# Order of the first layers and early casts in a retention and leaky-ReLU kernel

## The chip, the cores and the metric

The kernel runs on one core of a Trainium2 chip. Times are device microseconds of one execution; lower is better. Thirteen runs of the kernel before are shown, and one further look in detail, a profile of one of them. The engines are named as in the profile: PE multiplies matrices, DVE and POOL work elementwise, ACT does activations and copies, SP issues most of the transfers.

## What is computed

Two stages, one after the other. The first is a retention layer (attention without softmax): for each of 8 batches and 8 heads, with 576 positions and 64 channels,

```python
scores = scale * np.matmul(q, k.transpose(0, 1, 3, 2))
gamma = 1.0 - 2.0 ** (-5.0 - np.arange(H, dtype=np.float32))
Dmat = np.where(rel >= 0, gamma[:, None, None] ** rel[None, :, :], 0.0)
ret = scores * Dmat[None, :, :, :]
return np.matmul(ret, v)
```

Its output, seen as 4608 tokens of 512 channels, goes through two layers:

```python
h = x @ w_in                    # 512 -> 2048
g = np.maximum(0.01 * h, h)
return g @ w_out                # 2048 -> 512
```

Inputs and output are float32; the kernel multiplies in float16 and accumulates in float32.

## The kernel before

**Units and groups.** The 4608 tokens are 36 units of 128 tokens (two chunks of 64), and 9 groups of 512 tokens, four units each. A unit is what the retention stage works on; a group is what the two layers work on. Units 0 to 3 make group 0, units 4 to 7 group 1, and so on.

**A unit's life.** `load` (L119) fetches k, q and v, each 256 KB, into `t32` tiles, of which there are six for each of the three. `cast_k` (L170) rounds k to float16 on ACT; `cast_q` and `cast_v` (L174, L177) do so on DVE or POOL and multiply by the decay. q and k are then transposed, into `qkT`: either on PE with a copy out (`turn`, L624: `transpose_pe` and `transposed`), or by a DMA that SP issues (`transpose_dma`, L181). `scores` (L209) issues 64 small matmuls into one PSUM tile, `sc`: the scores and, beside them, each chunk's contribution to the running state. DVE masks the scores (`masks`) and adds the state to what is carried from chunk to chunk (`state`); `state_cast` rounds it, on DVE, ACT or POOL as the caller says.

**Two forms of a unit's output.** `outputs` (L283) puts the part inside a chunk and the part from the state into two halves of an `ot` tile; `own` (L353) copies the first half on ACT, and `add` (L359) adds the second to it on DVE, into the unit's 128 columns of `xT`, the input of the first layer. `outputs_acc` (L309) lets PE accumulate both parts in one half of the tile, with a drain of PE between its two rounds, and `x_copy` (L340) brings it to `xT` by one copy on ACT. There is one `ot` tile and one `sc` tile.

**The first layer** makes 16 blocks of 128 hidden channels for each group, through one of four `acc` accumulators, and ACT applies the leaky ReLU from there into `gt`. The blocks come in three shapes: `h_block` (L389), 512 tokens at a time; `h_half(g, a, fb)` (L394), two blocks for the half `a` of the tokens, and `halves` calls it for a list of (a, fb); `h_unit(u, fb)` (L401), four blocks for one unit alone. They let the first layer of groups 0 and 1 begin before all four units are there.

**The second layer.** Group 0 uses `wide` (L419), four PE calls of 16 matmuls for each 128 tokens. Groups 1 to 8 use `seven` (L469): a product by halves with seven multiplications instead of eight, as in Strassen's and Winograd's scheme. It needs differences of the weights (`mix_weights`, L440, once for all groups) and sums of the activations (`mix`, L455, parts 0 to 3 for each group), all on DVE. In `seven` p1 is a sum of two products in one accumulator; between the two, ACT copies p1 out (`keep`, L492, into `k1`), and p6 plus k1 gives u2, from which the rest follows. `give` (L499) writes an output half, and its store follows.

**Order.** Nothing is reordered: each engine runs its instructions in the order in which the source issues them. That order is written out by hand:

- the opening (L558 to L613): transfers are issued by SP and POOL; then units 0 to 3, each with `scores`, state, masks, the transposes of the next unit, and for units 0 to 2 the output. `keep_warm` (L546) issues matmuls on zeros, whose result nobody reads.
- groups 0 and 1 of the first layer (L639 to L693), with units 4 to 7 between their blocks.
- group 0 of the second layer (L751 to L754), during which the retention of units 8 and 9 runs: `burst` (L700) issues the scores of a unit and the outputs of the unit before it, `ahead` (L715) the casts and the DMA transpose of a later unit, and `early` (L734) a burst, an `ahead` three units on and a `load` five units on. The dictionary `at` says after which of the 16 `wide` calls each comes.
- `early(10)`, the last sums of group 1, and `seven(1, ...)` with `early(11)` after its first product and `early(12)` after its fifth.
- groups 2 to 8 (L761 to L776), with a `step` (burst, load, `ahead`) at four fixed places of each.

SP issues its transfers in the order of the source as well: the transpose of unit u stands between loads of later units. `load(8)` waits for the third of four transfers of `w_out`.

Of the kernel before, what the change touches and what calls it, by code (L numbers as in the profile page):

```python
# [18 lines left out]
def kernel(  # L19
# [125 lines left out]
    def load_w_in(f, after=None):  # L145
        fs = slice(f * FQ, (f + 1) * FQ)
        rows = moe_w_in.rearrange("(o c k) f -> o k c f", o=2, k=CH)
        ds = []
        for o in range(2):
            ds.append(nc.gpsimd.dma_start(out=w_in16[half(o), :, fs], in_=rows[o][:, :, fs]))  # L150
            if after is not None and not o:
                behind(ds[0], *after)
        return ds
# [16 lines left out]
    def cast_k(u):  # L170
        qk16[u] = a_pool.tile([P, 2, H, D], F16, name="qk16")
        nc.scalar.copy(out=qk16[u][:, 1], in_=t32[u, 1])  # L172
# [167 lines left out]
    def x_copy(u):  # L340
        nc.scalar.copy(  # L341
            out=x_of(u), in_=ot_tiles[u][:, 0].rearrange("q (c j) t -> q c (j t)", j=2)
        )
# [125 lines left out]
    def seven(g, hooks, last=False):  # L469

        r = {}
        s = sums[g]

        def product(name, lhs, rhs, fresh):
            if fresh:
                r[name] = acc_pool.tile([P, 2, HN], FP, name="acc")
            order = (
                [(f, tb) for tb in range(2) for f in range(HF)]
                if last
                else [(f, tb) for f in range(HF) for tb in range(2)]  # L480
            )
            for n, (f, tb) in enumerate(order):
                nc.tensor.matmul(  # L483
                    out=r[name][:, tb, :],
                    lhsT=lhs[:, f, tb * P : (tb + 1) * P],
                    rhs=rhs[:, f, :],
                    start=fresh and n == 0,
                    stop=f == HF - 1,
                    skip_group_check=True,
                )  # L490

        def keep(name, of, plus=None):  # L492
            r[name] = m_pool.tile([P, 2, HN], FP, name=name)
            if plus is None:
                nc.scalar.copy(out=r[name], in_=r[of])  # L495
            else:
                nc.vector.tensor_tensor(out=r[name], in0=r[of], in1=r[plus], op=ADD)

        def give(a, b, of, plus=None, parts=1):  # L499
            if ("o", a) not in r:  # L500
                r["o", a] = o_pool.tile([P, 2, DM], FP, name="osb")
            for n in range(parts):
                ts = slice(n * 2 // parts, (n + 1) * 2 // parts)
                to = r["o", a][:, ts, b * HN : (b + 1) * HN]
                if plus is None:
                    nc.scalar.copy(out=to, in_=r[of][:, ts])
                else:
# [12 lines left out]
            if r["n", a] == 2 and not (last and a == 1):  # L520
                store(g, a, r["o", a])

        plan = (
            ("p1", g_part(g, 0, 0), w_part(0, 0), True, lambda: keep("k1", "p1")),
            ("p1", g_part(g, 0, 1), w_part(1, 0), False, lambda: give(0, 0, "p1")),
            ("p6", s[:, 1], w_mix[:, 1], True, lambda: keep("u2", "p6", "k1")),
            ("p5", s[:, 0], w_mix[:, 0], True, lambda: keep("v", "p5", "u2")),
            ("p7", g_part(g, 1, 0), w_mix[:, 2], True, lambda: give(1, 1, "p7", "v")),
            ("p5", g_part(g, 0, 0), w_part(1, 1), False, lambda: give(0, 1, "p5", "u2")),
            (  # L530
                "p7", g_part(g, 1, 1), w_mix[:, 3], False,
                lambda: give(1, 0, "p7", "u2", 2 if last else 1),
            ),
        )
        for n, (name, lhs, rhs, fresh, then) in enumerate(plan):
            product(name, lhs, rhs, fresh)
            then()
            if n == 0:
                mix(g, 3, 0)
                mix(g, 3, 1)  # L540
            for f in hooks.get(n, ()):
                f()
# [17 lines left out]
    load(1, {1: nc.sync, 0: nc.gpsimd, 2: nc.gpsimd})  # L560
    load(2, nc.gpsimd)
    load(3, {1: nc.sync, 0: nc.gpsimd, 2: nc.gpsimd}, {1: (last_load[1, 1],)})
    for f in range(3):
        load_w_in(f)
    load(4, nc.gpsimd)
    load_w_in(3)
    for u in range(5, 8):
# [14 lines left out]
    for u in range(4):  # L582
        n = u + 1
        scores(u)
        if not u:
            keep_warm(3)
        state(u, 0)
        state_cast(u, dve_copy, (0,))
        masks(u)
        if not u:  # L590
            cast_q(1, nc.vector)
            cast_v(1, nc.vector)
        state(u, 1)
        if n < 4:
            transpose_pe(n, 1)
            transposed(n, 1, act_copy)
            if not u:
                keep_warm(3)
                outputs_acc(0)
                x_copy(0)  # L600
                keep_warm(1)
            transpose_pe(n, 0)
            transposed(n, 0, act_copy)
            keep_warm(2 if not u else 3)
        if n < 3:
            cast_k(n + 1)
            cast_q(n + 1, nc.vector)
            cast_v(n + 1, nc.vector)
        state_cast(u, act_copy, (1,))
        if 0 < u < 3:  # L610
            outputs_acc(u)
            x_copy(u)
            keep_warm(2)  # L613


    def halves(g, *items):
        for a, fb in items:
            h_half(g, a, fb)

    def cast_qv(u):  # L620
        cast_q(u, nc.vector)
        cast_v(u, nc.vector)

    def turn(u, x):  # L624
        transpose_pe(u, x)
        transposed(u, x, dve_copy)

    def settle(u):
        state(u, 0)
        state_cast(u, dve_copy, (0,))  # L630
        masks(u)
        state(u, 1)

    def finish(u):
        outputs_acc(u)
        x_copy(u)
        state_cast(u, act_copy, (1,))

    halves(0, (0, 0), (0, 1))  # L639
    outputs_acc(3)  # L640
    x_copy(3)
    halves(0, (0, 2), (0, 3), (1, 0))
    cast_k(4)
    cast_qv(4)
    halves(0, (1, 1), (1, 2), (1, 3))
    turn(4, 1)
    halves(0, (0, 4), (0, 5))
    turn(4, 0)
    halves(0, (1, 4), (1, 5))
    cast_k(5)  # L650
    scores(4)
    settle(4)
    cast_qv(5)
    halves(0, (0, 6), (0, 7))
    finish(4)
    turn(5, 1)
    cast_k(6)
    halves(0, (1, 6))
    turn(5, 0)
    halves(0, (1, 7))  # L660
    scores(5)
    settle(5)
    cast_qv(6)
    h_unit(4, 0)
    turn(6, 1)
    cast_k(7)
    h_unit(4, 1)
    finish(5)
    turn(6, 0)
    h_unit(5, 0)  # L670
    scores(6)
    settle(6)
    cast_qv(7)
    h_unit(5, 1)
    turn(7, 1)
    halves(1, (0, 4))
    finish(6)
    turn(7, 0)
    halves(1, (0, 5))
    scores(7)  # L680
    settle(7)
    halves(1, (0, 6), (0, 7))
    finish(7)
    load(8, after=(w_out_loads[2],))
    load(9)
    h_unit(6, 0)
    mix_weights(0, 0)
    mix_weights(0, 1)
    h_unit(7, 0)
    for n in range(1, 4):  # L690
        mix_weights(n, 0)
        mix_weights(n, 1)
        halves(1, (1, 2 * n), (1, 2 * n + 1))  # L693

    def mixes(g, *ns):
        for n in ns:
# [34 lines left out]
        ahead(u + 2)  # L731


    def early(u, out=True):  # L734
        burst(u, out)
        if 8 < u < 12:
            ahead(u + 3)
            load(u + 5)

    ahead(8)  # L740
    load(10)
    ahead(9)
    load(11)
    at = {
        2: lambda: (ahead(10), load(12)),
        4: lambda: (burst(8, False), ahead(11), load(13)),
        9: lambda: early(9),
        11: lambda: mixes(1, 0),
        13: lambda: mixes(1, 1),
    }  # L750
    for n in range(16):  # L751
        wide(n // 4, n % 4)
        if n in at:
            at[n]()  # L754
    early(10)
    mixes(1, 2)
    seven(1, {0: [lambda: early(11)], 4: [lambda: early(12)]})

    first = [f for i in range(4) for f in (i, i + HF)]
# [47 lines left out]
```

## Time and profile before

| | us |
|---|---|
| median of 13 runs | 301.19 |
| lowest and highest run | 296.9, 302.9 |
| the profiled execution | 302.66 |
| its span, first to last instruction | 300.9 |

All 13 runs, sorted: 296.9, 297.45, 298.21, 298.23, 299.72, 299.99, 301.19, 301.35, 301.48, 302.36, 302.64, 302.66, 302.9.

The page of the profiled execution opens with the busy time of each engine:

```profile
PE 285.3 (95%) x4096; PEld 193.7 (64%) x4096; DVE 169.6 (56%) x291; ACT 144.0 (48%) x254; POOL 103.8 (34%) x124
```

PEld is the load of weights, which overlaps PE's matmuls. Where the time of PE goes, by stretches of the span:

| stretch, us | what runs on PE | PE busy, us | mean clock | DMA share |
|---|---|---|---|---|
| 0 to 20 | opening: units 0 to 3, fillers | 15.99 | 1.00 | 1.02 |
| 20 to 50 | first layer of group 0, units 4 to 7, part of group 1 | 28.17 | 1.00 | 1.05 |
| 50 to 60 | first layer of group 1 | 9.91 | 1.00 | 0.34 |
| 60 to 70 | second layer of group 0, units 8 and 9 | 9.86 | 1.00 | 0.95 |
| 70 to 80 | the same, unit 10, first product of group 1 | 6.46 | 0.97 | 1.16 |
| 80 to 90 | unit 11, second layer of group 1 | 8.87 | 0.69 | 1.08 |
| 90 to 100 | the same, unit 12 | 10.00 | 1.00 | 1.14 |
| 100 to 284 | groups 2 to 8 | full | 1.00 | 0.10 to 1.09 |
| 284 to 301 | last second layer | 12.26 | 1.00 | 0.17 |

The clock is the share of full speed that was granted to PE; the DMA share is the mean busy share of the core's 16 DMA engines.

What one operation takes, from the groups of instructions: a first-layer matmul of 512 columns 0.216 us one after the other (64 in 13.81 us), of 256 columns 0.109, of 128 columns 0.056; an activation, a copy or a cast of 128 x 512 on ACT 0.58 to 0.62; an elementwise product of that size on DVE 0.68, on POOL 1.04; one load of 256 KB lands 3.8 to 5.1 us after its issue, one DMA transpose 3.2.

The chain of work that ended last, by engine:

```profile
PE 86%; DMA 5%; POOL 2%; SPq 2%; issue 2%; ACT 1%; DVE 1%; DVEq 0%; ACTq 0%; POOLq 0%
```

"SPq" is SP's queue of transfers; "issue" is time in which an engine waited for nothing that the profile shows.

### The profile page before, as it was taken

How to read it: one execution, taken by the hardware profiler on the slowest of the kernel's cores; microseconds unless marked ns; L12 is line 12 of the kernel's file. 1: busy time of each engine (PE TensorE's matmuls, PEld its weight loads, DVE VectorE, ACT ScalarE, POOL GpSimd, SP SyncE). 2: the span in 40 equal slices, each digit the busy share in tenths (PEclk: the TensorE clock that was granted, in tenths of full speed). 3: DMA queues.
4: the chain of work that ended last, by engine and by line, in shares of the span. 5: the costliest groups of instructions: out<-in, count | busy, mean ns of one | idle time of the engine just before them, and what ended most of it. 6: DMA issues, size and time to landing. Idle time of an engine off the chain costs nothing.

```text
span 300.9 us, 9407 instructions
## 1 busy us (share of the span) xinstructions
PE 285.3 (95%) x4096; PEld 193.7 (64%) x4096; DVE 169.6 (56%) x291; ACT 144.0 (48%) x254; POOL 103.8 (34%) x124
## 2 busy tenths in 40 slices
PE   7799989999499999999999999999999999999994
PEld 2468878745387458646864686478547844884583
DVE  2862469717925358555746664577358636740342
ACT  4547756712412762376147624761575166306510
POOL 8859503324442333333334333333334514000000
PEclk9999999999779999999999999999999999999999
DMA  8999999199999975996698767967896361012003
GB/s 222 272 240 240 239 198 200 26 190 202 165 297 228 285 154 133 219 237 136 132 246 196 181 143 219 178 156 171 220 215 139 69 176 37 4 45 97 0 2 139
DMA packets 132219, 50.01 MB, mean 166 GB/s; under 512 B 121777, under 2 KB 126513, under 8 KB 132177
## 3 DMA queue, kind: packets, MB, share of 16 engines
q1 hardware_dynamic: 125904, 39.73, 58.4%
q0 software_dynamic: 5984, 9.57, 14.4%
q8 instruction: 32, 0.52, 0.7%
q10 hardware_dynamic: 288, 0.11, 0.1%
q14 instruction: 11, 0.08, 0.1%
HBM read 36.81 MB, written 9.44 MB: 154 GB/s over the span
## 4 chain that ended last, share of the span: by engine, by line
PE 86%; DMA 5%; POOL 2%; SPq 2%; issue 2%; ACT 1%; DVE 1%; DVEq 0%; ACTq 0%; POOLq 0%
PE acc L373 42%; PE acc L483 33%; DMA t<-in_v_dram 4%; PE sc L215 3%; POOL t L132 2%; DMA t<-in_k_dram 1%; PE acc L423 1%; PE ot L321 1%; PE sc L224 1%; SPq L183 1%; PE ot L291 1%; PE ot L302 1%; PE acc L200 1%; SPq L132 1%; PE ot L333 1%
## 5 line engine op out<-in xcount | busy, mean ns | idle before, releaser
L373 PE MATMUL acc<-xT,w_in 128*128 128x512 f16 (+2 forms) x752 | 130.7, 329 | 0.6 <-ACT xT L341 0.3
L387 ACT ACTIVATE gt<-acc 128x512 f16<-128x512 f32 x144 | 85.9, 597 | 57.5 <-PE acc L373 56.0
L373 PEld LDWEIGHTS <-w_in 128*128 128x128 f16 x752 | 68.0, 98 | 52.4 <-issue 0.9
L483 PEld LDWEIGHTS <-gt 128*128 128x128 f16 x640 | 62.6, 99 | 11.7 <-issue 1.8
L233 DVE TENSOR_TENSOR s<-sc,cs 128x512 f16<-128x512 f32 x36 | 24.7, 685 | 43.9 <-PE sc L224 43.9
L483 PE MATMUL acc<-w_out,gt 128*128 128x256 f16 x384 | 47.6, 279 | 1.8 <-ACT k L495 1.6
L273 POOL CAST st<-s 128x512 f16<-128x512 f32 x21 | 13.7, 653 | 83.3 <-DVE s L257 53.7
L175 POOL TENSOR_TENSOR qk<-t,cs 128x512 f16<-128x512 f32 x28 | 29.3, 1047 | 33.3 <-DMA t<-in_q_dram 31.9
L355 ACT COPY own<-ot 128x512 f32<-128x512 f32 x28 | 16.4, 586 | 38.5 <-PE ot L302 31.2
L179 POOL TENSOR_TENSOR v<-t,cs 128x512 f16<-128x512 f32 x28 | 31.8, 1134 | 4.9 <-DMA t<-in_v_dram 4.4
L172 ACT CAST qk<-t 128x512 f16<-128x512 f32 x36 | 22.2, 620 | 21.6 <-DMA t<-in_k_dram 17.0
L483 PE MATMUL acc<-w_mix,gt 128*128 128x256 f16 x256 | 30.6, 273 | 0.0
L467 DVE TENSOR_TENSOR mix<-gt 128x1024 f16<-128x1024 f16 x16 | 14.0, 878 | 28.8 <-ACT gt L387 28.8
L483 PE MATMUL acc<-w_mix,mix 128*128 128x256 f16 x256 | 29.5, 274 | 0.0
L483 PEld LDWEIGHTS <-mix 128*128 128x128 f16 x256 | 25.2, 99 | 3.1
L360 DVE TENSOR_TENSOR xT<-ot,own 128x512 f16<-128x512 f32 x28 | 19.1, 682 | 1.6 <-ACT own L355 1.6
L257 DVE TENSOR_TENSOR s<-sc,s 128x256 f32<-128x256 f32 x40 | 16.7, 418 | 3.7 <-PE sc L224 2.6
L215 PEld LDWEIGHTS <-qkT 64*64 64x64 f16 x576 | 7.8, 108 | 15.1 <-issue 9.1
L508 DVE TENSOR_TENSOR osb<-acc,u 128x512 f32<-128x512 f32 (+1 forms) x17 | 11.1, 655 | 8.0 <-PE acc L483 8.0
L215 PE MATMUL sc<-qkT 64*64 64x64 f16 x576 | 11.6, 199 | 3.5 <-DMA qkT<-qk 3.1
L467 DVE TENSOR_TENSOR mix<-mix,gt 128x1024 f16<-128x1024 f16 x16 | 14.4, 905 | 0.5
L423 PE MATMUL acc<-w_out,gt 128*128 128x512 f16 x64 | 14.3, 379 | 0.0
(52 smaller groups left out, 234.4 us busy)
## 6 DMA issues: line engine op xcount, KB each, us to landing
out_dram<-osb SPq DMA_DIRECT2D x17, 512.0 KB, 3.7
t<-in_k_dram SPq DMA_DIRECT2D x28, 256.0 KB, 3.8
t<-in_q_dram SPq DMA_DIRECT2D x25, 256.0 KB, 4.1
t<-in_v_dram SPq DMA_DIRECT2D x25, 256.0 KB, 5.1
w_in<-in_moe_w_in_dram POOLq DMA_DIRECT2D x8, 256.0 KB, 7.2
w_out<-in_moe_w_out_dram POOLq DMA_DIRECT2D x4, 512.0 KB, 11.2
t<-in_v_dram POOLq DMA_DIRECT2D x7, 256.0 KB, 5.4
t<-in_q_dram POOLq DMA_DIRECT2D x6, 256.0 KB, 5.3
```

Source lines behind the costliest of these rows:

```text
L172: nc.scalar.copy(out=qk16[u][:, 1], in_=t32[u, 1])
L175: eng.tensor_tensor(out=qk16[u][:, 0], in0=t32[u, 0], in1=decay(u, 0), op=MUL)
L179: eng.tensor_tensor(out=v16[u], in0=t32[u, 2], in1=decay(u, 1), op=MUL)
L215: nc.tensor.matmul(out=a[half(j), g, 0, p, :], lhsT=qkT[u][half(g), 1, p, half(j)], rhs=qkT[u][half(g), 0, p, half(j)], start=True, stop=T ...
L233: nc.vector.tensor_tensor(out=s16s[u], in0=sc_tiles[u][:, :, 0], in1=mask_sb.unsqueeze(1).unsqueeze(1).to_broadcast([P, 2, NP, CH]), op=MUL,)
L257: nc.vector.tensor_tensor(out=to, in0=st, in1=carry[0], op=ADD)
L360: nc.vector.tensor_tensor(out=x_of(u).rearrange("q (c g) t -> q c g t", g=2), in0=ot_tiles[u][:, :, NP : 2 * NP].rearrange("q g (c j) t -> ...
L373: nc.tensor.matmul(out=hps[:, n, :], lhsT=w_in16[:, c, f * P : (f + 1) * P], rhs=xT[g][:, c, ts], start=(c == 0), stop=(c == NP - 1),)
L387: nc.scalar.activation(out=out, in_=in_, func=mybir.ActivationFunctionType.Lrelu)
L423: nc.tensor.matmul(out=ys[tb], lhsT=g_t[0][:, f, tb * P : (tb + 1) * P], rhs=w_out16[:, f, :], start=(f == 0), stop=(f == NF - 1),)
L467: nc.vector.tensor_tensor(out=z[:, fs], in0=a[:, fs], in1=b[:, fs], op=op)
L483: nc.tensor.matmul(out=r[name][:, tb, :], lhsT=lhs[:, f, tb * P : (tb + 1) * P], rhs=rhs[:, f, :], start=fresh and n == 0, stop=f == HF - ...
```

## The change

Five things are changed.

1. In the last group's `seven`, p6 is computed second, between the two products of p1.
2. In the opening, the two `keep_warm` matmuls after the outputs of unit 2 are left out. The loop is written with other conditions, and the order of what remains is the same.
3. Units 3 and 4 use `outputs`, `own` and `add` (a new function `finish2`) in place of `outputs_acc` and `x_copy`. Units 5 to 7 keep `finish`.
4. In the first layers of groups 0 and 1 the steps of units 4 to 7 stand at other places: `scores(4)` after `halves` (0, 4) instead of after (1, 5), the outputs of unit 4 three half blocks earlier, `cast_k(6)` after `settle(5)`, `finish(7)` after `h_unit(6, 0)`. Two half blocks of group 1, (1, 2) and (1, 3), become `h_unit(6, 1)` and `h_unit(7, 1)`.
5. `ahead(8)`, `load(10)`, `ahead(9)` and `load(11)` move from after the first layer of group 1 to between its last blocks, and `ahead(10)` with `load(12)` one `wide` call up. The sums 0, 1 and 2 of group 1 move from after the `wide` calls 11, 13 and the burst of unit 10 to after the calls 0, 3 and 7.

```diff
+        if last:
+            plan = (plan[0], plan[2], plan[1]) + plan[3:]
         for n, (name, lhs, rhs, fresh, then) in enumerate(plan):
...
-        if 0 < u < 3:
-            outputs_acc(u)
-            x_copy(u)
+        if u == 1:
+            outputs_acc(1)
+            x_copy(1)
             keep_warm(2)
+        elif u == 2:
+            outputs_acc(2)
+            x_copy(2)
...
+    def finish2(u):
+        outputs(u)
+        own(u)
+        add(u)
...
     halves(0, (0, 0), (0, 1))
-    outputs_acc(3)
-    x_copy(3)
+    finish2(3)
     halves(0, (0, 2), (0, 3), (1, 0))
     cast_k(4)
     cast_qv(4)
-    halves(0, (1, 1), (1, 2), (1, 3))
+    halves(0, (1, 1), (1, 2))
     turn(4, 1)
-    halves(0, (0, 4), (0, 5))
+    halves(0, (1, 3))
     turn(4, 0)
-    halves(0, (1, 4), (1, 5))
-    cast_k(5)
+    halves(0, (0, 4))
     scores(4)
     settle(4)
+    halves(0, (0, 5), (1, 4))
+    finish2(4)
+    state_cast(4, act_copy, (1,))
+    halves(0, (1, 5))
+    cast_k(5)
     cast_qv(5)
     halves(0, (0, 6), (0, 7))
-    finish(4)
     turn(5, 1)
-    cast_k(6)
     halves(0, (1, 6))
     turn(5, 0)
     halves(0, (1, 7))
     scores(5)
     settle(5)
+    cast_k(6)
     cast_qv(6)
...
     halves(1, (0, 6), (0, 7))
-    finish(7)
     load(8, after=(w_out_loads[2],))
     load(9)
     h_unit(6, 0)
+    finish(7)
+    h_unit(6, 1)
     mix_weights(0, 0)
     mix_weights(0, 1)
     h_unit(7, 0)
-    for n in range(1, 4):
-        mix_weights(n, 0)
-        mix_weights(n, 1)
-        halves(1, (1, 2 * n), (1, 2 * n + 1))
...
+    h_unit(7, 1)
+    mix_weights(1, 0)
+    mix_weights(1, 1)
+    halves(1, (1, 4))
+    ahead(8)
+    load(10)
+    mix_weights(2, 0)
+    mix_weights(2, 1)
+    halves(1, (1, 5), (1, 6))
+    ahead(9)
+    load(11)
+    mix_weights(3, 0)
+    mix_weights(3, 1)
+    halves(1, (1, 7))
...
-    ahead(8)
-    load(10)
-    ahead(9)
-    load(11)
     at = {
-        2: lambda: (ahead(10), load(12)),
+        0: lambda: mixes(1, 0),
+        1: lambda: (ahead(10), load(12)),
+        3: lambda: mixes(1, 1),
         4: lambda: (burst(8, False), ahead(11), load(13)),
+        7: lambda: mixes(1, 2),
         9: lambda: early(9),
-        11: lambda: mixes(1, 0),
-        13: lambda: mixes(1, 1),
     }
...
     early(10)
-    mixes(1, 2)
     seven(1, {0: [lambda: early(11)], 4: [lambda: early(12)]})
```

The functions `mixes`, `burst`, `ahead`, `fetch` and `step` are moved up in the file, unchanged.

More of the change, by code (lines that the diff above doesn't have):

```diff
@@ L562 @@
     load(3, {1: nc.sync, 0: nc.gpsimd, 2: nc.gpsimd}, {1: (last_load[1, 1],)})
-    for f in range(3):
-        load_w_in(f)
+    load_w_in(0)
+    load_w_in(1)
+    load_w_in(2)
     load(4, nc.gpsimd)
@@ L603 @@
             transposed(n, 0, act_copy)
-            keep_warm(2 if not u else 3)
+            keep_warm(3 if u else 2)
         if n < 3:
@@ L637, in finish @@
         state_cast(u, act_copy, (1,))
-    halves(0, (0, 0), (0, 1))
-    outputs_acc(3)
-    x_copy(3)
-    halves(0, (0, 2), (0, 3), (1, 0))
-    cast_k(4)
-    cast_qv(4)
-    halves(0, (1, 1), (1, 2), (1, 3))
-    turn(4, 1)
-    halves(0, (0, 4), (0, 5))
-    turn(4, 0)
-    halves(0, (1, 4), (1, 5))
-    cast_k(5)
[L651 to L654, printed above, removed]
-    finish(4)
-    turn(5, 1)
-    cast_k(6)
[L658 to L682, printed above, removed]
-    finish(7)
[L684 to L689, printed above, removed]
-    for n in range(1, 4):
-        mix_weights(n, 0)
-        mix_weights(n, 1)
-        halves(1, (1, 2 * n), (1, 2 * n + 1))
+    def finish2(u):
+        outputs(u)
+        own(u)
+        add(u)
     def mixes(g, *ns):
@@ L731, in step @@
         ahead(u + 2)
+    halves(0, (0, 0), (0, 1))
+    finish2(3)
+    halves(0, (0, 2), (0, 3), (1, 0))
+    cast_k(4)
+    cast_qv(4)
+    halves(0, (1, 1), (1, 2))
+    turn(4, 1)
+    halves(0, (1, 3))
+    turn(4, 0)
+    halves(0, (0, 4))
+    scores(4)
+    settle(4)
+    halves(0, (0, 5), (1, 4))
[3 more added lines that the diff above has]
+    cast_k(5)
+    cast_qv(5)
+    halves(0, (0, 6), (0, 7))
+    turn(5, 1)
+    halves(0, (1, 6))
+    turn(5, 0)
+    halves(0, (1, 7))
+    scores(5)
+    settle(5)
+    cast_k(6)
+    cast_qv(6)
+    h_unit(4, 0)
+    turn(6, 1)
+    cast_k(7)
+    h_unit(4, 1)
+    finish(5)
+    turn(6, 0)
+    h_unit(5, 0)
+    scores(6)
+    settle(6)
+    cast_qv(7)
+    h_unit(5, 1)
+    turn(7, 1)
+    halves(1, (0, 4))
+    finish(6)
+    turn(7, 0)
+    halves(1, (0, 5))
+    scores(7)
+    settle(7)
+    halves(1, (0, 6), (0, 7))
+    load(8, after=(w_out_loads[2],))
+    load(9)
+    h_unit(6, 0)
+    finish(7)
+    h_unit(6, 1)
+    mix_weights(0, 0)
+    mix_weights(0, 1)
+    h_unit(7, 0)
+    h_unit(7, 1)
[12 more added lines that the diff above has]
+    halves(1, (1, 7))
     def early(u, out=True):
```

## The prediction

> **What bounds the kernel now.** The page's first part comes first: PE is busy 285.3 us of a 300.9 us span (95%), so time is won where PE idles or is slowed, or where it does work the result doesn't need. The slices (7.5 us each, part 2) show where:
>
> ```profile
> PE   7799989999499999999999999999999999999994
> ...
> PEclk9999999999779999999999999999999999999999
> DMA  8999999199999975996698767967896361012003
> ```
>
> There are three low places: slices 0 to 5 (the opening), slice 10 with a low clock in slices 10 and 11 (75 to 90 us), and the last. DMA falls to 1 in slice 7 (52.7 to 60.2 us) and is full from slice 8: a hole just ahead of a shortage. Next the waits of PE after 60 us:
>
> ```profile
> PE sc L215 <- DMA qkT<-qk: 3.1, 1, 3.1
> PE acc L483 <- ACT k L495: 1.6, 2, 0.9
> PE ot L302 <- POOL st L273: 0.6, 2, 0.4
> ```
>
> That is nearly all PE waits for until the end; from 100 us on each group takes 29.1 us without a gap. PE's timeline places the 3.1:
>
> ```profile
> 79.96 0.43 PE L215 MATMUL sc<-qkT 64*64 64x64 f16 x16 [3.11 <-DMA qkT<-qk]
> ...
> 82.37 3.57 PE L483 MATMUL acc<-w_out,gt 128*128 128x256 f16 x16 [0.92 <-ACT k L495]
> ```
>
> The first is scores(11), waiting for unit 11's transpose. The second is p1's second product, which can't accumulate before ACT has copied p1 (`keep k1`). It took 3.57 us where sixteen of that shape take 1.92 elsewhere: clock 0.50 from 80 to 86 us by the two-microsecond windows. The chain of waits says why both are late:
>
> ```profile
> 66.83 5.49 DMA t<-in_v_dram
> ...
> 73.62 1.08 POOL st L273
> ...
> 76.69 4.43 DMA t<-in_k_dram
> ...
> 81.22 0.63 ACT qk L172
> ```
>
> SP, ACT and DMA carry it: k of unit 13 lands at 81.1, cast_k(13) stands on ACT ahead of k1's copy. SP's timeline has where this string of transposes (T) and loads (L) begins:
>
> ```profile
> 59.60 1.33 SPq L183 DMA_TRANSPOSE qkT<-qk  x1
> 61.03 0.53 SPq L132 DMA_DIRECT2D t<-in_k_dram  x1
> ```
>
> T8 59.6, L10 61.0, T9 63.2, L11 65.6, T10 68.3, L12 71.3, T11 74.1, L13 75.9: SP hardly rests in between, since each transfer takes 0.5 to 2.9 us to issue and DMA is full. T8 started only when ACT had cast k(8), and ACT shows that cast after the last activation:
>
> ```profile
> 58.42 0.60 ACT L387 ACTIVATE gt<-acc 128x512 f16<-128x512 f32 x1 [0.28 <-PE acc L373]
> 58.92 1.13 ACT L172 CAST qk<-t 128x512 f16<-128x512 f32 x2
> ```
>
> Unit 8's q had landed at 49.7 (POOL casts it there). So the whole string is about six microseconds later than its data allowed, because of its place in ACT's and SP's order.
>
> **What the Trainium skill says.** "TensorE: Matmul & The Clock Gate", section "What's actually happening": PE's clock is halved after an idle window of about 3.4 us and restored after as long a busy one. The trace agrees in kind, and 3.11 us of waiting were enough here: clock 0.50 from 80 to 86, back at 1.00 from 88. "DMA: Bandwidth & Descriptors", section "Issuing engines are not separate DMA queues": all queues share 16 DMA engines. The trace agrees in that share is about 1.0 from 64 us on; so the string can be started earlier, hardly run faster. "GPSIMD Engine Reference", section "1. Specifications": its SBUF interface is shared with VectorE. The trace agrees: the pair of w_mix subtractions under POOL's casts took 2.98 us, the last pair alone 1.28.
>
> **The change part by part.** The sum is made on the profiled execution: 302.66 us, span 300.9 and 1.76 around it.
>
> *(a) Fillers after outputs 2.* Two keep_warm matmuls go, 18.66 to 19.20: 0.53 us of PE. scores(3) starts at about 18.6; its inputs are ready (qkT copies end at 17.7, the sc bank is read out at 18.0). The first chunk of w_in had landed by 17 (POOL's waits on it), so first blocks start at 19.0, not 19.5.
>
> *(b) Plain outputs for 3 and 4.* outputs_acc(4) holds PE 34.26 to 35.03, 0.77 us with its drain; `outputs` takes 0.26 (a burst's 64 matmuls 0.64, less 0.38 for scores). Saved 0.5 each. But xT is then made by own on ACT (0.59) and add on DVE (0.69) in place of one 0.59 copy. For unit 4 many blocks cover that: 0.5 stays. For unit 3 it does not. ACT's queue (state cast, two activations, copy) hangs on scores(3): before, x_copy ended at 23.68; now own ends at about 23.15, add at 23.9. PE reaches block (1,0), the first that reads unit 3, at 19.0 + 1.85 + 0.26 + 1.75 = 22.85 and waits 1.1 us. It started (1,0) at 24.07 before, 23.95 now: of 1.0 us saved by (a) and unit 3, 0.1 is left.
>
> *(c) Order of units 4 to 7.* scores(4) and outputs(4) move up by three half blocks; cast_k(4) ends at 26.0 and q(4) at 25.6, ahead of their turns at 26.6 and 27.7. cast_k(6) now follows the last activation of group 0, and turn(6,1) may wait up to 0.15 us: I take 0.1. h_unit(6,1) and (7,1) replace two halves: 16 x 0.056 against 8 x 0.109, equal. finish(7) is one unit later, with the same 0.9 us block over its copy. In all (a) to (c): 0.1 + 0.5 - 0.1 = **0.5 us**. The 0.87 and 0.26 us gaps without a releaser in this stretch I leave as they are.
>
> *(d) Casts of 8 and 9 between blocks.* `ahead(8)` now comes after the fifth of eight blocks, three of 0.875 us earlier: T8 at 57.0 in PE's old time instead of 59.6, 2.6 us. ahead(9) comes one block before the end, done by 58.7, before T9's turn (60.6). Loads 8 and 9 don't change place; SP has issued them by 51.1, and load 8's wait for the third w_out transfer stays. ACT holds the sixth activation 0.3 us longer; four accumulators cover it. T8 also waits for POOL's cast_q(8), done at 50.8. In the string every L and T after that moves with T8: T11 lands at 77.3 (79.9), k(13) at 78.5 (81.1).
>
> *(e) mix 0 to 2 of group 1 earlier.* Six DVE instructions leave 71.5 to 79.1 for 59 to 66, where DVE had 3 us of work in 10 and POOL little: PE time 0. masks(8) at 63.1 come after the 2.6 us of the first four; if contention stretches these as it did w_mix they end near 63, still in time.
>
> Then PE: st(9) on POOL stood behind v(11) and held PE 0.43; moved by 2.6 this goes, and PE asks for scores(11) at 76.4. It waits until 77.3 (0.85), for st(10) until 78.4 (0.6), for k1, which stays behind cast_k(13), until 79.7 (1.1). p1's second product starts at 79.72 instead of 82.37: **2.65 us**. What is late next is still k(13). As no gap nears a window, I take the clock to stay up: before, that product lost 1.65 and p6 0.25, so **1.9 us**. If it still halves, 0; if stalls were short already, less.
>
> *(f) Last group, p6 second.* p1's second product waited 0.72 for k1. p6 needs the second sum, ready at 285.95 on DVE; PE starts at 286.05 instead of 286.34: **0.3 us**.
>
> Sum: 0.5 + 2.65 + 1.9 + 0.3 = 5.35; 302.66 - 5.35 = 297.3. The runs shown go from 296.9 to 302.9, median 301.19, 1.5 below the profiled one. No trace shows what varies; I suppose half is this stall, and take 0.8 off: **296.5 us**.
>
> **The rivals.**
> *Fully hidden.* If the string gets through faster (it has an idle DMA in front of it), the remaining 2.5 us of waits go as well: 297.3 - 2.5 = 294.8. For it: T took 1.3 us to issue when DMA was calm, 2.9 when full. Against: its data are the same.
> *No gain at the stall.* The string is limited by completions, not by its start, or the clock halves all the same: (d) pays 0 to 1, the rest 0.8: 301.19 - 0.8 - 0.5 = 299.9, within 1%. Against: DMA moved nothing from 54 to 60.
> *Slower, in the opening.* With fillers gone and 1.1 us of idleness ahead of (1,0), the clock halves at 23: 3.4 to 7 us at half speed cost 1.7 to 3.5, the wait 1.1, and if (d) pays nothing then 301.2 + 3 = 304. It decides once the gaps between 18.6 and 24 fill most of a window. Against: before, at 12 to 14, PE had 1.14 us of work in 2 and kept its clock.
> *Not what it says:* the built order shows ahead(8) between activations and SP's order unchanged, so I give this nothing.
>
> **How the numbers follow.** Likeliest 0.52 (296.5, from 295 to 298.2), fully hidden 0.22, no gain 0.18, slower 0.08. About 1% is what a measurement of this kernel tells from no change: 298.2 and 304.2. Faster by over 1%: 0.52 x 0.95 + 0.22 + 0.02 for part of the third, about 0.73; within: 0.21; slower 0.06. The range leaves out the slow case and the ends of the others: 293.9 to 299.6.
>
> **What would show it.** T8 should start about 3 us before the block that ends the first layer does, scores(11) wait under 1 us, PE's clock stay at 9 in all slices, k1's wait be the last left near 79. Block (1,0) should show about 1 us of waiting on DVE's add. In the last group the wait for k1 should be gone. I am wrong if T11 lands as late after T8 as PE arrives, or if a new low clock shows near 23 us.

## The result, and the profile after

| | us |
|---|---|
| changed kernel, median of 11 runs | 294.56 |
| its lowest and highest run | 293.08, 296.91 |
| the kernel before, median of 48 runs | 300.63 |
| ratio, 95% interval | 0.9845 (0.9812 to 0.9879) |
| the profiled execution of the changed kernel | 292.49 (span 290.7) |

The median is 6.1 us lower, which is a ratio of 0.980. The ratio in the table comes out nearer to 1, since it leaves out slow runs, those more than 1.5% above the fastest of their kernel: 15 of the 48 of before and one of the changed kernel. The two profiled executions lie 10.2 us apart, since that of before was one of its longer ones and that of the changed kernel is shorter than all 11 runs. So the two traces together overstate the change, and the sum below is checked against several traces of each kind.

The slices of the changed kernel, tenths of each 7.3 us:

```profile
PE   8898999999999999999999999999999999999994
...
PEclk9999999999999999999999999999999999999999
DMA  7999998699999998966697669889986151012003
```

The low place of PE in slice 10 is gone, and so is the low clock. DMA's hole is a 6 where it was a 1. What PE still waits for after 17 us, in this execution:

```profile
PE acc L373 <- DVE xT L360: 0.8, 1, 0.8
PE acc L373 <- ACT xT L341: 0.3, 1, 0.3
PE ot L321 <- ACT qkT L207: 0.3, 1, 0.3
PE acc L200 <- issue: 0.2, 1, 0.2
```

Neither scores(11), which waited 3.11 us before, nor k1 is in the list; the first line is block (1, 0), which waits for unit 3's add. SP's timeline has the string of transposes and loads (T8 is the transpose of unit 8, and so on):

```profile
54.62 1.32 SPq L183 DMA_TRANSPOSE qkT<-qk  x1
56.05 0.53 SPq L132 DMA_DIRECT2D t<-in_k_dram  x1
...
68.06 1.75 SPq L183 DMA_TRANSPOSE qkT<-qk  x1
```

T8, the first of these lines, is issued at 54.6, and T11, the last, at 68.1. PE begins group 0's second layer at 55.9, so T8 stands 1.24 us ahead of that, where it stood 1.38 behind: 2.62 us earlier. Here are ACT and PE at the place where p1's second product was slow before:

```profile
73.65 0.62 ACT L172 CAST qk<-t 128x512 f16<-128x512 f32 x1 [1.07 <-DMA t<-in_k_dram]
74.17 0.58 ACT L495 COPY k<-acc 128x512 f32<-128x512 f32 x1
```

```profile
74.81 1.91 PE L483 MATMUL acc<-w_out,gt 128*128 128x256 f16 x16
```

cast_k(13) still waits for its load and k1's copy still stands behind it, but both are over when PE gets there. In other executions of the same kernel they are not, as will be seen.

### The profile page after: what moved, and what is told of

Same layout as the page of the kernel before. It is cut to its first block, busy times and chain, and to the rows that moved or that the text cites. A ratio compares the mean times of both kernels' runs of the same rounds, so it can differ in the third digit from the quotient of the medians.

```text
span 290.7 us, 9446 instructions
## 1 busy us (share of the span) xinstructions
PE 282.0 (97%) x4118; PEld 192.2 (66%) x4118; DVE 169.5 (58%) x293; ACT 143.9 (49%) x254; POOL 103.4 (36%) x124
## 4 chain that ended last, share of the span: by engine, by line
PE 92%; DVE 4%; ACT 1%; DMA 1%; issue 1%; DVEq 0%
PE acc L373 42%; PE acc L483 34%; PE acc L423 5%; PE sc L215 3%; PE sc L224 2%; PE ot L291 1%; PE ot L302 1%; DMA t<-in_k_dram 1%; PE acc L200 1%; PE ot L321 1%; DVE s L233 1%; PE acc L551 1%; DVE s L257 1%; DVE xT L360 0%; DVE v L179 0%
## 5 line engine op out<-in xcount | busy, mean ns | idle before, releaser
L483 PEld LDWEIGHTS <-gt 128*128 128x128 f16 x640 | 61.9, 98 | 9.3
L483 PE MATMUL acc<-w_out,gt 128*128 128x256 f16 x384 | 45.9, 273 | 0.3
L273 POOL CAST st<-s 128x512 f16<-128x512 f32 x21 | 12.8, 609 | 82.6 <-DVE s L257 53.7
L175 POOL TENSOR_TENSOR qk<-t,cs 128x512 f16<-128x512 f32 x28 | 30.2, 1078 | 29.1 <-DMA t<-in_q_dram 23.1
L355 ACT COPY own<-ot 128x512 f32<-128x512 f32 x30 | 17.6, 585 | 36.7 <-PE ot L302 29.3
L467 DVE TENSOR_TENSOR mix<-gt 128x1024 f16<-128x1024 f16 x16 | 14.8, 922 | 30.6 <-ACT gt L387 30.6
L179 POOL TENSOR_TENSOR v<-t,cs 128x512 f16<-128x512 f32 x28 | 31.0, 1108 | 1.3 <-DMA t<-in_v_dram 1.3
L360 DVE TENSOR_TENSOR xT<-ot,own 128x512 f16<-128x512 f32 x30 | 20.4, 681 | 4.2 <-ACT own L355 4.2
L276 POOL CAST st<-s 128x256 f16<-128x256 f32 x7 | 3.2, 454 | 30.8 <-DVE s L261 17.4
L467 DVE TENSOR_TENSOR mix<-mix,gt 128x1024 f16<-128x1024 f16 x16 | 13.1, 826 | 0.5
```

Of the source, the lines that this page charges most:

```text
L175: eng.tensor_tensor(out=qk16[u][:, 0], in0=t32[u, 0], in1=decay(u, 0), op=MUL)
L179: eng.tensor_tensor(out=v16[u], in0=t32[u, 2], in1=decay(u, 1), op=MUL)
L355: nc.scalar.copy(out=owns[u], in_=ot_tiles[u][:, :, 0:NP].rearrange("q j c t -> q c j t"))
L360: nc.vector.tensor_tensor(out=x_of(u).rearrange("q (c g) t -> q c g t", g=2), in0=ot_tiles[u][:, :, NP : 2 * NP].rearrange("q g (c j) t -> ...
L467: nc.vector.tensor_tensor(out=z[:, fs], in0=a[:, fs], in1=b[:, fs], op=op)
L483: nc.tensor.matmul(out=r[name][:, tb, :], lhsT=lhs[:, f, tb * P : (tb + 1) * P], rhs=rhs[:, f, :], start=fresh and n == 0, stop=f == HF - ...
```

## The experiments

**Two distances** are used throughout, so that the scatter of the opening and the length of the span don't enter. The first runs from the start of group 0's second layer (W) to the start of p1's second product: it holds all waits for the string of transposes and loads. The second runs from there to scores(12): with a full clock that is 7.1 us of matmuls without a wait (7.07 to 7.10 in ten rows), so what it has above that is the clock's cost.

| kernel | T8 after W (minus: before it), us | T8 to T11 | W to p1's second | from there to scores(12) |
|---|---|---|---|---|
| before | +1.38 | 14.47 | 24.15 | 8.96 |
| before_again | +1.38 | 12.87 | 22.12 | 8.74 |
| before_filled | +1.38 | 13.13 | 23.12 | 7.08 |
| first_layers_only | +1.38 | 13.02 | 22.01 | 7.08 |
| all_but_early | +1.38 | 13.57 | 22.01 | 7.08 |
| early_only | -1.24 | 13.40 | 19.12 | 7.09 |
| changed | -1.24 | 13.44 | 18.95 | 7.07 |
| changed_again | -1.24 | 13.79 | 20.86 | 7.08 |
| late_sums | -1.24 | 13.00 | 20.64 | 8.63 |
| acc_for_3 | -1.24 | 13.32 | 20.41 | 8.75 |
| fillers_back | -1.24 | 14.04 | 20.65 | 7.08 |
| k1_first | -1.23 | 13.92 | 18.74 | 7.10 |
| three_more | -3.01 | 13.01 | 18.76 | 7.09 |
| three_other | -3.01 | 13.41 | 18.62 | 7.09 |

Each row is one traced execution, so differences of up to two microseconds in the first distance can be scatter: changed and changed_again, the same kernel, lie 1.9 us apart.

**early_only: the early casts without the rest.** On the kernel before:

```diff
-    for n in range(1, 4):
-        mix_weights(n, 0)
-        mix_weights(n, 1)
-        halves(1, (1, 2 * n), (1, 2 * n + 1))
+    mix_weights(1, 0)
+    mix_weights(1, 1)
+    halves(1, (1, 2), (1, 3), (1, 4))
+    ahead(8)
+    load(10)
...
+    halves(1, (1, 5), (1, 6))
+    ahead(9)
+    load(11)
...
+    halves(1, (1, 7))
...
-    ahead(8)
-    load(10)
-    ahead(9)
-    load(11)
...
-        2: lambda: (ahead(10), load(12)),
+        1: lambda: (ahead(10), load(12)),
```

> The kernel before with part 5 alone, without its sums: ahead(8) and load(10) after half block (1, 4), ahead(9) and load(11) after (1, 6), ahead(10) one wide call up; all else as before. My theory (the string of transposes and loads starts at cast_k(8), and its start decides): first transpose 2.6 us earlier relative to the end of group 1's first layer, p1's second product waits under 1.5 us in all, clock 1.00 throughout, median about 4 us under that of before (ratio 0.985 to 0.99). Rival 1 (the string runs at the pace of its transfers, whatever its start): scores(11) wait as long as before, ratio 0.997 to 1.00. Rival 2 (the gain sits in the opening and the first layers): ratio 0.997 to 1.00 as well, but with the wait at scores(11) shorter by 2 us.

Measured: median 295.5 us against 300.31, ratio 0.9813 (0.9745 to 0.9882), clock 1.00 in the trace; one of the four runs still took 300.27, at a mean clock of 0.989. The lines show T8 on SP, then scores(11), the outputs of unit 10 behind the add of unit 9, and p1's second product on PE:

```profile
55.68 1.33 SPq L183 DMA_TRANSPOSE qkT<-qk  x1
```

```profile
74.70 0.32 PE L215 MATMUL sc<-qkT 64*64 64x64 f16 x16
...
75.67 0.32 PE L291 MATMUL ot<-s,v 64*64 64x64 f16 x16 [0.52 <-DVE xT L360]
...
76.04 1.92 PE L483 MATMUL acc<-w_out,gt 128*128 128x256 f16 x16
```

T8 is 2.62 us earlier, the string takes 13.4 us as elsewhere (12.9 to 14.5 in all rows, whatever its start), and p1's second product comes 3 to 5 us sooner, without a wait for scores(11) or k1. Rival 1 falls: the string's start decides. Rival 2 falls as the only source of the gain; first_layers_only below shows that the first layers have a gain of their own.

**all_but_early: everything except that.** On the changed kernel:

```diff
-    ahead(8)
-    load(10)
...
-    ahead(9)
-    load(11)
...
+    ahead(8)
+    load(10)
+    ahead(9)
+    load(11)
     at = {
...
-        1: lambda: (ahead(10), load(12)),
+        2: lambda: (ahead(10), load(12)),
```

> The changed kernel with ahead(8), load(10), ahead(9), load(11) back behind the first layer of group 1 and ahead(10) back after wide call 2; opening, first layers, early sums and p6 second in the last group stay. My theory: the wait of 3 us at scores(11) and the low clock come back in most runs, ratio to before 0.995 (1 to 1.5 us for opening and last group), 3 us over the changed kernel. Rival 1 or 2 (not the start of the string): about as fast as the changed kernel, ratio 0.985.

Measured: median 295.75, ratio 0.9855 (0.9792 to 0.9919). My theory expected 0.995, so it missed, and by its ratio the rival was right. But the waits did come back. The two longest lines of PE's waits after 18 us:

```profile
PE sc L215 <- DMA qkT<-qk: 2.5, 2, 1.3
PE acc L483 <- ACT k L495: 1.0, 1, 1.0
```

They make 3.5 us, as much as in before_again below (3.4). What did not come back, in this trace, is the low clock: the waits stand in three pieces of 1.0 to 1.3 us, at scores(9), at scores(11) and at k1, and the second distance is 7.08. Of the four runs one has a mean clock of 0.994, the others 0.997 or more. So the stall has two costs, the waiting and the clock after it, and the second mostly goes when the longest gap is broken up. Against the usual 20.4 to 20.9 us of the changed kernel's first distance the waits cost 1.1 to 1.6 us here, which is about the difference of the medians (295.75 and 294.56, of different sets of runs).

**first_layers_only: the opening and the first layers alone.** all_but_early with the sums and the last group's order as before as well:

```diff
-        0: lambda: mixes(1, 0),
-        3: lambda: mixes(1, 1),
-        7: lambda: mixes(1, 2),
+        11: lambda: mixes(1, 0),
+        13: lambda: mixes(1, 1),
...
+    mixes(1, 2)
...
-        if last:
-            plan = (plan[0], plan[2], plan[1]) + plan[3:]
```

> The changed kernel with the casts back behind the first layer, the sums back at their old places, and the last group in its old order: what stays is the opening without two fillers, plain outputs for units 3 and 4, and the new order of the first layers. My theory: group 0's second layer starts 0.5 us earlier, the wait at scores(11) is unchanged or longer by as much, ratio 0.997 to 1.00. Rival 2: ratio 0.988 or less. A rival of its own: PE idles about 1 us ahead of block (1, 0) and the clock falls near 23 us, ratio over 1.005.

Measured: median 296.92, ratio 0.9891 (0.9837 to 0.9945): 3.4 us, where I expected up to 1. That is close to what rival 2 forecast (0.988 or less). No low clock near 23 us, so the rival that forecast a loss there falls. The two longest lines of PE's waits:

```profile
PE acc L483 <- ACT k L495: 2.5, 2, 1.8
PE sc L215 <- DMA qkT<-qk: 1.3, 1, 1.3
```

The row of the table says where the gain comes from: the same T8, the same 22.0 us to p1's second product as before_again (22.12), but 7.08 us after it; all four runs have a mean clock of 1.00. With W about 0.8 us earlier (counted from scores(2), as below) and the clock's cost gone (1.7 to 1.9), some 2.6 of the 3.4 us are accounted for; the rest is not placed.

**late_sums: the sums of group 1 back at their old places.**

```diff
-        0: lambda: mixes(1, 0),
-        3: lambda: mixes(1, 1),
-        7: lambda: mixes(1, 2),
+        11: lambda: mixes(1, 0),
+        13: lambda: mixes(1, 1),
...
+    mixes(1, 2)
```

> The changed kernel with the sums 0 to 2 of group 1 back after wide calls 11, 13 and the burst of unit 10. My theory: they cost PE 0.2 us at most, so the ratio to before is that of the changed kernel, 0.985. Rival 3 (DVE's queue was the late one: masks(10) and masks(11) stand behind the sums, and st(10) behind them): PE waits 1 to 2 us longer between scores(10) and p1's second product, ratio 0.988 to 0.992.

Measured: median 295.4, ratio 0.9835 (0.9787 to 0.9882), not to be told from the changed kernel. Its trace waits 1.96 us for k1, and changed_again below, with the early sums, waits 2.17. DVE does masks(11) at 77.0 in it, behind the sums, against 75.3 in the changed kernel's trace; but PE needs these masks only for outputs(11), several products later, so the delay stays on DVE. Rival 3 finds no support, but its 0.988 lies at the end of the interval: these four runs leave room for about a microsecond.

**before_filled: the gap filled, not shortened.** To tell the clock's cost from the waiting's, twelve matmuls on zeros went into the gap of the kernel before, ahead of scores(11):

```diff
-    seven(1, {0: [lambda: early(11)], 4: [lambda: early(12)]})
+    seven(1, {0: [lambda: (keep_warm(12), early(11))], 4: [lambda: early(12)]})
```

> The kernel before with twelve matmuls on zeros (2.6 us) between p1's first product of group 1 and scores(11), nothing else. They shorten no wait. If the clock's share of the loss is its own (the 3 us gap halves it for one or two windows), the mean clock is 1.00, and the time falls by 1.7 to 2 us, ratio 0.993 to 0.995, although PE still starts scores(11) when unit 11's transpose lands. If the low clock has another cause or costs nothing, ratio 1.00 or more, clock still 0.989 to 0.994.

Measured over 20 runs: median 298.64 against 301.05, ratio 0.9938 (0.9909 to 0.9967), mean clock 1.00 in the trace. That is 1.9 us won by work that nobody reads. In 17 of the 20 runs the clock is 0.997 or more and the time 296.6 to 299.3 us; in the other three it is 0.992 to 0.994, and they took 302. From the windows of two microseconds of before_again and of this kernel (columns: stretch; busy time and count of PE, PEld, DVE, ACT, POOL; clock; DMA share; GB/s), just after p1's second product starts:

```profile
80.00:82.00 2.00, 2.00 (x11) 1.40 (x10) 1.37 (x4) 0.00 (x0) 1.36 (x2) 0.50 0.97 319
```

```profile
80.00:82.00 2.00, 1.71 (x16) 1.53 (x16) 1.97 (x5) 0.73 (x2) 1.24 (x2) 1.00 1.01 321
```

At clock 0.50 PE is busy all the time and does 11 matmuls; at 1.00 it is busy for 1.71 us and does 16. Busy time alone would have suggested the opposite. The runs of the kernel before beside these, each with its mean clock, say the same: in 27 of them four have a clock of 0.999 or more and took 296.8 to 298.5 us, and the other 23, at 0.978 to 0.994, took 299.96 to 305.4.

**before_again: a second trace of the kernel before**, unchanged.

> The kernel before once more, for a second trace of it: ratio 1.00. If the profiled execution was typical, its waits at scores(11), st(10) and k1 add up to 4 to 5 us again and the clock falls after them; if it was an unlucky one, 2 to 3 us.

Measured: 299.28 us. The waits are 2.04 for scores(11), 0.28 for st(9) and none for st(10), 1.06 for k1: 3.4 us, between my two cases. The clock fell here too (second distance 8.74), after gaps of 2.04 and 1.06 us with 0.7 us between them.

**k1_first: k1's copy ahead of cast_k(13).** What may still be late in the changed kernel is k1, behind a cast whose load is late. On the changed kernel:

```diff
-    early(10)
-    seven(1, {0: [lambda: early(11)], 4: [lambda: early(12)]})
+    burst(10)
+    seven(
+        1,
+        {
+            0: [lambda: (burst(11), ahead(13), load(15), ahead(14), load(16))],
+            4: [lambda: early(12)],
+        },
+    )
```

> The changed kernel with ahead(13) and load(15) moved from before p1 to after burst(11), so that ACT copies k1 before it casts k of unit 13, which may not have landed. My theory (k1 behind cast_k(13) is what is left): the wait of p1's second product is under 0.3 us in the trace, the runs scatter less and their median falls by 0.5 to 1 us, ratio to before 0.979 to 0.983. Rival: the string is only moved, and T13 or unit 13's loads are late at scores(12) or (13): ratio 0.984 or more.

Measured: median 293.14, ratio 0.9796 (0.9717 to 0.9875), four runs from 292.8 to 293.5. No wait for k1 is left, and p1's second product comes 18.74 us after W. Units 12 and 13 are not late; scores(15) waits 0.28 us for its transpose, the only new wait.

**three_more: two further edits.** The edit of k1_first, and:

```diff
-    halves(0, (0, 2), (0, 3), (1, 0))
+    halves(0, (0, 2), (0, 3), (0, 4))
     cast_k(4)
     cast_qv(4)
-    halves(0, (1, 1), (1, 2))
+    halves(0, (1, 0), (1, 1))
     turn(4, 1)
-    halves(0, (1, 3))
+    halves(0, (1, 2))
     turn(4, 0)
-    halves(0, (0, 4))
+    halves(0, (1, 3))
     scores(4)
...
+    ahead(8)
+    load(10)
     h_unit(7, 1)
     mix_weights(1, 0)
     mix_weights(1, 1)
     halves(1, (1, 4))
-    ahead(8)
-    load(10)
```

> The changed kernel with that, and two more edits: half block (0, 4) of group 0 before (1, 0), so that own and add of unit 3 are covered; and ahead(8), load(10) one h_unit earlier, ahead of h_unit(7, 1). My theory: the 0.81 us wait at (1, 0) goes, the first transpose starts about 0.9 us earlier, no wait is left between 60 and 90 us: 1.3 to 2 us under the changed kernel, ratio to before 0.976 to 0.980. Rival: (0, 4) meets the third part of w_in before it has landed, and waits as long as (1, 0) did: ratio as k1_first.

Measured: median 292.77, ratio 0.9788 (0.9727 to 0.9849). The forecast of 0.9 us for the earlier start of T8 missed: T8 is another 1.8 us earlier. It buys nothing more once nobody waits for the string (18.76 us to p1's second product, against 18.74 in k1_first). The wait for add is gone, yet PE stands still for nearly as long at about the same time:

```profile
23.71 2.23 PE L373 MATMUL acc<-xT,w_in 128*128 128x256 f16 x19 [0.78 <-issue]
```

It stands in the middle of block (0, 4), after the fifth of eight matmuls, so it isn't the rival's wait for w_in either. The last section comes back to it.

**acc_for_3 and fillers_back** undo one part of the opening each, on the changed kernel; each has one traced run and no interval.

```diff
-    finish2(3)
+    outputs_acc(3)
+    x_copy(3)
```

> The changed kernel with the accumulated output and the one copy for unit 3 again. My theory (its plain output gains nothing, since block (1, 0) then waits for own and add): the two half blocks after it start 0.5 us later, (1, 0) waits under 0.2 us instead of 0.8, and scores(4) starts 0.1 to 0.3 us earlier, counted from scores(2). Rival (the shorter output is worth its 0.5 us): scores(4) starts 0.5 us later.

```diff
         elif u == 2:
             outputs_acc(2)
             x_copy(2)
+            keep_warm(2)
```

> The changed kernel with the two fillers after the outputs of unit 2 again. ACT's and DVE's chain to block (1, 0) hangs on scores(3), which moves by the fillers' 0.53 us: scores(4) starts 0.4 to 0.5 us later, counted from scores(2), and the wait at (1, 0) stays 0.8. Rival (the fillers kept the clock up): no low clock in either; rival (the wait at (1, 0) takes up the fillers): scores(4) where it was.

Six traces have the changed kernel's order from scores(2) to scores(4): changed 12.93 us, first_layers_only 12.97, all_but_early 13.0, late_sums 13.16, k1_first 13.33, changed_again 13.45. Without the gaps that are put down to "issue" they take 12.93 to 13.16. acc_for_3 takes 13.18, within the spread, so the forecast that scores(4) comes earlier did not show; 0.55 of it is such a gap, and without it 12.63 are left, with no wait for add. three_other below, with the same accumulated output, has 13.04 and 12.63. So unit 3's plain output gains nothing, and costs 0.3 to 0.5 us if those gaps are taken out. fillers_back takes 13.66, 0.2 to 0.7 more, and still waits 0.80 at (1, 0): the fillers were on the path, as far as one trace shows. Neither kernel has a low clock before 60 us.

**changed_again and three_other.** The changed kernel once more, and beside it k1_first with `ahead(8)` one block earlier and the accumulated output for unit 3 (the edits above, without the move of (0, 4)).

> The changed kernel once more, beside the next one on the same chip: ratio 0.982 to 0.987, its runs spread over 3 us or more, with k1's wait between 0.2 and 2 us.

> The changed kernel with k1's copy ahead of cast_k(13), ahead(8) and load(10) ahead of h_unit(7, 1), and the accumulated output for unit 3 in the place of half block (0, 4). My theory: 0.2 us under the kernel with the three other edits at best, ratio 0.976 to 0.981, and 1.5 us or more under the changed kernel beside it. Rival (what is left is transfers that scatter): not to be told from the changed kernel.

Measured: changed_again 294.48, ratio 0.9808 (0.9767 to 0.9849), six runs spread over 2.3 us, where I expected 3 or more. three_other 292.73, ratio 0.9745 (0.970 to 0.979), a little under the range expected, five runs spread over 0.9: 1.75 us under the changed kernel on the same chip, and the fastest here; three_more (292.77) and k1_first (293.14) can't be told from it. The longest waits of PE after 17 us, first of changed_again, then of three_other:

```profile
PE acc L483 <- ACT k L495: 2.2, 1, 2.2
PE acc L373 <- DVE xT L360: 0.8, 1, 0.8
```

```profile
PE acc L373 <- issue: 0.4, 1, 0.4
PE ot L333 <- issue: 0.4, 1, 0.4
PE acc L373 <- ACT xT L341: 0.3, 1, 0.3
```

The wait for k1 that the first trace of the changed kernel doesn't show is the usual one in kernels with its order: 1.6 to 2.2 us in changed_again, late_sums, acc_for_3 and fillers_back. It is what three_other has taken away.

## Why the prediction was right

The mechanism forecast is what early_only shows: the string of transposes started too late, and starting it sooner won back most of the waits and, in most executions, the clock after them. That the first layers alone win the clock back as well was not foreseen. The size came out less well than the ratio suggests. The forecast was 296.5 to 301.19, 0.984, and 0.9845 was measured, but that agreement is partly luck: over all runs the medians give 0.980. In microseconds the changed kernel came 1.9 under the point, within the range, but below the likeliest case (295 to 298.2) and next to the rival "fully hidden" (294.8). The traces show something between the two: the waits for scores(11) and st(10) are gone, as in that rival, and k1's wait is left in most executions. By the steps:

- **(a) and (b), opening.** The account of block (1, 0) held: a wait of 1.1 us on DVE's add was forecast, 0.80 or 0.81 is in every trace that has unit 3's plain output with (1, 0) in the changed kernel's place. The fillers were worth about their 0.53 (0.2 to 0.7 by the one trace that has them back), since the chain to (1, 0) hangs on scores(3), as said; plain output for unit 3 was put at nothing, and is worth nothing or costs up to 0.5. `scores` issues 32 small matmuls, 16 at each of its two lines, not the 64 named in its description; 64 is a whole burst, as (b) has it.
- **(a) to (c) together** were put at 0.5 us. From scores(2) to W the four traces with the old first layers take 41.5 to 42.4 us, the six with the changed kernel's opening and first layers (changed, changed_again, first_layers_only, all_but_early, late_sums, k1_first) 40.6 to 41.3. The means are 41.82 and 41.01: 0.8. The wait of 0.1 at turn(6, 1) was not seen, and the gaps without a releaser scatter from 0.2 to 1.1 in sum.
- **(d), the start of the string.** 2.6 us forecast, 2.62 measured, by taking three blocks off a time. The sign given for it, T8 about 3 us before the last block, does not follow from that sum, which puts T8 1.2 us before W (57.0 against 58.22); 1.24 was measured. The "about six microseconds" that the string was said to be late is the length of DMA's hole; by the cast of unit 8's q, done at 50.8, it was more than eight, but the sum makes no use of it. That the string runs at an unchanged pace held in every variant. p1's second product was to start 21.5 us after W (79.72 - 58.22); it started at 18.95 in the first trace of the changed kernel, and at 20.4 to 20.9 in its second and in late_sums, acc_for_3 and fillers_back. The waits for scores(11) (0.85) and st(10) (0.6) were forecast and aren't there, k1's (1.1) is larger, up to 2.2. T11 took 13.0 to 14.0 us after T8, where I carried the 14.5 of one long execution over.
- **The clock.** 1.9 us forecast, 1.9 by before_filled alone. It is gone from the changed kernel's two traces, not from every execution: of the 18 runs of changed and changed_again four have a mean clock of 0.992 to 0.994 and took 296.1 to 296.9 us. With waits for k1 of 1.65 to 2.2 us left, the second distance is 8.6 to 8.8 in late_sums and acc_for_3, but 7.08 in changed_again and fillers_back. So gaps of that size sometimes halve the clock. In late_sums it falls at 76.9, 1.8 us into the one wait for k1, far short of the window of about 3.4 us that the prediction reckoned with; that no gap would come near enough was too sure. In the 15 runs of k1_first, three_more and three_other, whose traces have no wait for k1, the clock is 0.997 or more.
- **(e), the sums.** PE time 0 forecast; late_sums can't be told from it.
- **(f), the last group.** This is the term that was mis-sized: 0.3 forecast, 0.74 measured, the same in every trace (p1 to the last addition 13.30 us before, 12.56 after). I had p6 wait for the whole second sum, but its first matmuls read the half of it that was ready before. The wait of before, then p6 and the second half of the sum in the changed kernel:

```profile
286.34 1.91 PE L483 MATMUL acc<-w_out,gt 128*128 128x256 f16 x16 [0.72 <-ACT k L495]
```

```profile
275.82 0.69 DVE L467 TENSOR_TENSOR mix<-mix,gt 128x1024 f16<-128x1024 f16 x1
```

```profile
276.01 2.04 PE L483 MATMUL acc<-w_mix,mix 128*128 128x256 f16 x16
```

p6 starts the moment p1 ends (276.01), with the second half of the sum under way until 276.5, so that the whole wait of 0.72 is won.
- **The step down to the median.** 0.8 us was taken off for the profiled run of before being a long one, on the guess that half its excess was the stall. With its second trace 2 us shorter up to p1's second product, more would have been right.

Put together again from the traces, as an estimate: 0.8 for (a) to (c); 2.8 for the first distance (means of 23.1 over before, before_again and before_filled and of 20.3 over changed, changed_again, late_sums, acc_for_3 and fillers_back); 1.2 for the clock (low in 23 of 27 runs of before and in 4 of 18 of the changed kernel, at 1.9 and 1.7 us); 0.74 for the last group. That is 5.5 of the 6.1 us.

The parts don't add up. Alone, the first layers give 3.4 us and the early casts 4.8; together, with sums and last group, 6.1. Much of the clock's 1.9 is in both, because either takes the one gap apart that causes it; the prediction counted it once. Why scores(9) waits in all_but_early and first_layers_only, and not in the kernel before, is settled only in part: T9 is issued 5.0 to 5.5 us after W in all of them, but lands 5.4 to 5.6 us after its issue in these two and 3.8 to 4.4 in before, before_again and before_filled. What slows it is open.

## What to carry to other kernels

Where a transfer engine stands idle just ahead of a shortage, look for what its first transfer waits for; here it was a cast of 0.6 us behind activations that had nothing to do with it. A gap of PE is priced with the clock after it, which can be measured by filling the gap with idle matmuls, and two edits that each break that gap up don't add. A small copy that PE waits for goes ahead of a cast whose data may be late; in-order queues make the one wait for the other.

## What was unexpected

PE stands still for 0.2 to 0.9 us, by "issue", at places that follow the count of instructions and not the work. Counted in the built order of PE's weight loads and matmuls, the first of these gaps comes after instruction 694 to 696 in before, three_more, three_other, acc_for_3 and changed_again, whether that is a matmul of block (1, 0) or of (0, 4). The second comes after 1202 in the kernels with the old first layers, in unit 5's output, and after 1458 to 1460 in the others, in or after unit 6's (in all_but_early it is put down to a copy on DVE). k1_first has one more, after 444. The distances are 250, 508 and some 765: once, twice and three times some 255.

The Trainium skill's "Runtime: NRT & Kernel Launch", section "Instruction fetch mechanics", has an engine's instructions fetched in blocks of 256 by transfers of its own, at a cost that is "mostly hidden". The page of each traced execution lists 32 packets of such transfers; that of the changed kernel reads:

```profile
q8 instruction: 32, 0.52, 0.7%
```

They are of 16 KB each, and the 4096 weight loads and 4096 matmuls of the kernel before are 32 times 256. By the times of the packets in the traces, each of the 20 gaps (19 by "issue", and that of all_but_early) ends 1.2 to 1.6 us after one of them has landed: the first packet of the span for the gap after 444, the second for 694 to 696, the fourth for 1202, the fifth for 1458 to 1460. So the gaps are very likely fetches that come late while DMA is full (its share is 1.05 from 20 to 50 us in before), and "mostly hidden" agrees as far as at most two of 32 packets show. That is a match in time; no run moved a fetch to test it.

It would explain why removing the 0.81 us wait in three_more brought nothing. In the changed kernel's first trace the second packet lands at 21.72, so that by this distance PE could go on at 22.9 to 23.3 (an estimate); the wait for add ends at 23.24, and PE would have stood there anyway.
